# Bucket attention and two dense layers: S and the transposes of P in tiles of 64 rows

## Chip, cores and metric

The kernel runs on 1 core of one Trainium2 chip. The metric is the device time of one execution in microseconds; lower is better.

## What is computed

Attention in which a query sees only the keys of its own hash bucket, over 2 batches of 8 heads, 768 positions, head width 64; then two dense layers of width 512 and 2048. Cut to what matters:

```python
q_bits = (np.einsum('bhsd,dk->bhsk', q, proj) > 0)        # 6 bits a query, 6 a key
k_bits = (np.einsum('bhsd,dk->bhsk', k, proj) > 0)
mask   = q_bucket[:, :, :, None] == k_bucket[:, :, None, :]
scores = np.where(mask, q @ k.T / 8, -1e9)
attn   = softmax(scores); x = attn @ v                    # heads side by side: 1536 x 512
g1 = h1 * clip(h1 + 3, 0, 6) / 6, h1 = x @ w_in1;   y1 = g1 @ w_out1
g2 = h2 * tanh(softplus(h2)),     h2 = y1 @ w_in2;  out = g2 @ w_out2
```

## The kernel before

Matmul operands that must be exact to about float32 are split into a high and a low part (type fp32r) and multiplied in three products; the transposes of P and P·V take plain float32.

Attention goes over 8 pairs of heads, each with 12 *units*: 128 queries of one head against all 768 keys, 96 units in all (NU). `attention_step` (L726) writes out by hand, in program order, two units a step; every engine works through its own instructions in that order. One unit n goes through

- **S** (`emit_S`, L634): scores into two PSUM banks, one for each half of 384 keys. Each half takes two products: the first has 128 contraction rows (QA holds the high over the low part of q, KA twice the high part of k), the second 76 (QB the high part of q over 12 rows of bits, KX the low part of k over 12 rows of bits). The bits add a penalty of at least 2^30 where buckets differ. Two such pairs of banks exist, s0 and s1.
- **min** on VectorE (`emit_min`), **exp** with its sum on ScalarE (`emit_exp`), then, for four units at once, statistics on VectorE (`emit_stats`) and the normalising of P on GpSimd (`emit_norm`).
- **T** (`emit_T`, L676), L = 6 units later: six transposes of 128 x 128, three to bank t0 and three to t1; the copies to SBUF (`emit_tevac`, L690) are shared by ScalarE and VectorE.
- **P·V** (`emit_pv`, L695), 12 units later: two heads as two column tiles of 64; then the result is split into xh and xl.

A step's order on TensorE is P·V, T, S, T, S. Seen from the first T, that is T, S, T, S, P·V. `prep` (L535) makes the operands of the next pair meanwhile: high parts on GpSimd (`prep_hi`), bits by four column tiles of 32 (`prep_z`), low parts, and moves from SBUF to SBUF on SyncE's DMA queue. Lines 547 to 621 and `late_prep` are the ramp of the first pair, `busy` matmuls fill gaps there. After step n = 94 six drain steps (L806) run the last T and P·V with the first matmuls of the dense layers (`mid`) between; `HERE` (L801) is how many weight slots are opened beside attention. From there on `moe_step` runs the dense layers.

Of the kernel before, what the change touches and what calls it, by code (L numbers as in the profile page):

```python
# [20 lines left out]
def bucket_attention_two_moe_kernel(  # L21
# [50 lines left out]
    pz = const.tile([128, 32], F32, name="pz")  # L72
    c8 = const.tile([128, 8], F32, name="c8")
# [189 lines left out]
    with tc.manual_schedule():  # L263
# [153 lines left out]
        with ExitStack() as actx:  # L417
            v_p = actx.enter_context(tc.tile_pool(name="v", bufs=2, side="right"))
            p_p = actx.enter_context(tc.tile_pool(name="p", bufs=6, side="right"))
            t0_p = actx.enter_context(tc.tile_pool(name="pt0", bufs=3, side="right"))  # L420
            t1_p = actx.enter_context(tc.tile_pool(name="pt1", bufs=4, side="right"))
# [5 lines left out]
            QA = [[big.tile([128, S], F32R, name=f"qa{i}{h}") for h in range(2)] for i in range(2)]  # L427
            KA = [[big.tile([128, S], F32R, name=f"ka{i}{h}") for h in range(2)] for i in range(2)]
            QB = [[big.tile([128, S], F32R, name=f"qb{i}{h}") for h in range(2)] for i in range(2)]
            KX = [[big.tile([128, S], F32R, name=f"kb{i}{h}") for h in range(2)] for i in range(2)]  # L430
            raw_t, vn_t, bit_t, hi_t = {}, {}, {}, {}

# [4 lines left out]
            def load_first(nm):  # L437
                raw_t[0, nm] = first_tile(nm)
                nc.sync.dma_start(out=raw_t[0, nm].bitcast(F32), in_={"k": k, "q": q}[nm][0, :2].rearrange("h d s -> (h d) s"))


            def load(p):
                if p < NPAIR:
                    b, hp = divmod(p, H // 2)
                    for nm, src in (("k", k), ("q", q)):
                        t = qk_p.tile([128, S], F32R, tag=nm, name=nm)
                        nc.sync.dma_start(out=t.bitcast(F32), in_=src[b, 2 * hp:2 * hp + 2].rearrange("h d s -> (h d) s"))
                        raw_t[p, nm] = t
# [7 lines left out]
            def prep_z(p):  # L456
                if p == 0:
                    bit_t[p] = first_tile("bits")[:, :HALF]
                else:
                    bit_t[p] = qk_p.tile([128, HALF], F32R, tag="bits", name="bits")  # L460
                ps = bank("m")
                for g in range(4):
                    hf, c = divmod(g, 2)
                    P.matmul(ps[32 * g:32 * g + 32, :HALF], lhsT=pz,  # L464
                             rhs=raw_t[p, "kq"[c]].bitcast(F32)[:, hf * HALF:(hf + 1) * HALF],
                             start=True, stop=True, tile_position=(0, 32 * g))
                V.tensor_scalar(out=bit_t[p], in0=ps[:, :HALF], scalar1=0.0, scalar2=cvec,
                                op0=ALU.is_gt, op1=ALU.not_equal)

            lo_, hi_ = slice(0, 64), slice(64, 128)  # L470
            halves = [slice(0, HALF), slice(HALF, S)]
# [31 lines left out]

# [4 lines left out]
            def prep_bits(p, heads=(0, 1), groups=range(4), queue=nc.sync):  # L508
                for h in heads:
                    for g in groups:  # L510
                        hf, c = divmod(g, 2)
                        move((KX, QB)[c][p % 2][h][64:64 + NZ, hf * HALF:(hf + 1) * HALF],
                             bit_t[p][32 * g + 16 * h:32 * g + 16 * h + NZ], queue)

            def prep_q_lo(p):
                qr = raw_t[p, "q"]
                V.scalar_tensor_tensor(out=qr, in0=qr.bitcast(F32), scalar=-0.125, in1=hi_t[p][1].bitcast(F32),
                                       op0=ALU.mult, op1=ALU.subtract)
# [28 lines left out]
            load_first("k")  # L547
            with nc.allow_non_contiguous_dma(reason="tiny"):
                nc.scalar.dma_start(out=pz[lo_, :NB], in_=proj)
            load_first("q")  # L550
            A.preload_act_table_set("natural_log_exp_and_others")
            for rows, cols in ((lo_, slice(NZ, 32)), (hi_, slice(0, 16)), (hi_, slice(16 + NZ, 32))):
# [3 lines left out]
            for g in range(4):  # L556
                V.memset(kbig[32 * g:32 * g + 32], (BIG, 1.0)[g % 2])
            for g in range(8):
                o = 16 * g + (0, NB)[g // 2 % 2]
# [305 lines left out]
```

## Time and profile before

| | us |
|---|---|
| median of 3 runs | 761.95 (761.87 to 763.3) |
| profiled execution, span | 759.9 |
| first T (step n = 6) begins | 19.13 |
| steady steps, n = 12 to 94 | 32.62 to 220.86 |
| drain steps | 220.86 to 246.9 |
| dense layers alone | 246.9 to 759.9 |

How to read it: an engine's busy time in a stretch is the sum of its instructions there, overlaps counted once. The records of TensorE's matmuls overlap, since each includes its way through the array; the distance from one start to the next is what a matmul costs in a stream. "PEld" are the weight loads, which run beside the matmuls. The chain gives the time to the engine on which the end of the program hung in turn.

### The profile page before, as it was taken

The page shows a single profiled execution, that of the slowest core. Times are in us where ns is not written, and L with a number is a line of the kernel's source. Part 1 is how long each engine was busy: PE and PEld are TensorE (multiplying, and loading weights), DVE is VectorE, ACT ScalarE, POOL GpSimd, SP SyncE. Part 2 cuts the span into 40 slices and gives each one's busy share as a digit, 9 for nine tenths or more (in the row PEclk, how much of TensorE's full clock was granted, in tenths as well). Part 3 has the DMA queues.
Part 4 walks back from the last instruction along what each step waited for, and adds up shares of the span by engine and source line. Part 5 has one row for each costly group of instructions (what it writes and reads, how often), then busy time and mean ns, then how long its engine had stood idle before and what let it go on. Part 6 is the DMA issues. An engine that isn't in the chain of part 4 may idle for free.

```text
span 759.9 us, 10494 instructions
## 1 busy us (share of the span) xinstructions
PE 749.7 (99%) x3754; PEld 586.9 (77%) x3754; DVE 482.1 (63%) x907; ACT 424.1 (56%) x787; POOL 135.9 (18%) x136
## 2 busy tenths in 40 slices
PE   8899999999999999999999999999999999999997
PEld 6666666666666888888888888888888888888886
DVE  6777787787778997968566257676554756121212
ACT  6677787677868885766555245644444444222221
POOL 4666556566540000000000000000000000000000
PEclk9999999999999999999999999999999999999999
DMA  6655474665202433223212001212112110010101
GB/s 173 177 145 149 142 190 119 177 188 140 89 29 84 139 112 110 88 80 125 69 56 84 1 0 58 83 55 84 56 55 84 56 55 1 1 55 1 55 1 57
DMA packets 23236, 65.04 MB, mean 86 GB/s; under 512 B 3840, under 2 KB 5072, under 8 KB 23184
## 3 DMA queue, kind: packets, MB, share of 16 engines
q1 hardware_dynamic: 22960, 64.23, 27.5%
q8 instruction: 30, 0.49, 0.3%
q14 instruction: 22, 0.18, 0.1%
q10 hardware_dynamic: 224, 0.13, 0.1%
HBM read 42.99 MB, written 3.15 MB: 61 GB/s over the span
## 4 chain that ended last, share of the span: by engine, by line
PE 95%; DVE 2%; ACT 1%; DMA 0%; issue 0%; POOL 0%; SPq 0%; DVEq 0%; ACTq 0%; POOLq 0%
PE s L343 33%; PE t L290 17%; PE pv L290 9%; PE t L687 9%; PE s L642 8%; PE m L290 7%; PE m L700 5%; PE pv L700 4%; PE m L464 1%; PE s L290 1%; PE t L343 1%; PE m L343 1%; DVE st L650 1%; DMA q<-in_q_dram 0%; DVE pt L475 0%
## 5 line engine op out<-in xcount | busy, mean ns | idle before, releaser
L322 DVE TENSOR_TENSOR gl<-gr,gh 128x512 fp32r<-128x512 f32 x96 | 66.1, 689 | 116.6 <-PE s L343 85.1
L673 POOL TENSOR_SCALAR p<-p,st 128x768 f32<-128x768 f32 x96 | 98.0, 1036 | 75.9 <-PE t L687 34.3
L656 ACT ACTIVATE p<-s,st 128x768 f32<-128x768 f32 x96 | 86.7, 903 | 29.7 <-DVE st L650 26.8
L650 DVE TENSOR_REDUCE st<-s 128x1 f32<-128x768 f32 x96 | 91.5, 954 | 15.2 <-PE s L642 11.5
L318 ACT CAST gh<-gr 128x512 fp32r<-128x512 f32 x96 | 59.6, 621 | 61.9 <-PE s L343 37.5
L687 PEld LDWEIGHTS t<-ident,p 128*128 128x128 f32 x576 | 63.1, 140 | 37.4 <-issue 17.2
L687 PE MATMUL t<-ident,p 128*128 128x128 f32 x576 | 82.5, 278 | 2.9 <-ACT pt L474 1.7
L290 PE MATMUL t<-xh,wih 128*128 128x512 f32 x192 | 75.0, 390 | 0.0
L343 PE MATMUL s<-gh,woh 128*128 128x512 f32 x192 | 74.9, 390 | 0.0
L474 ACT COPY pt<-t 128x384 f32<-128x384 f32 x121 | 57.4, 476 | 31.1 <-PE t L687 30.5
L290 PE MATMUL t<-xl,wih 128*128 128x512 f32 x192 | 74.8, 389 | 0.0
L343 PE MATMUL s<-gh,wol 128*128 128x512 f32 x192 | 74.7, 389 | 0.0
L290 PE MATMUL t<-xh,wil 128*128 128x512 f32 x192 | 74.7, 389 | 0.0
L343 PE MATMUL s<-wol,gh 128*128 128x512 f32 x176 | 68.5, 389 | 0.0
L343 PE MATMUL s<-woh,gh 128*128 128x512 f32 x176 | 68.5, 389 | 0.0
L642 PE MATMUL s<-ka,qa 128*128 128x384 f32 x192 | 57.7, 382 | 0.4 <-DVE qa L481 0.3
L475 DVE COPY pt<-t 128x384 f32<-128x384 f32 x71 | 39.3, 554 | 29.2 <-PE t L687 29.2
L143 DVE SCALAR_TENSOR_TENSOR raw<-raw 128x512 uint32<-128x512 uint32 x64 | 44.1, 688 | 16.9 <-ACT raw L139 16.9
L642 PE MATMUL s<-kb,qb 76*128 76x384 f32 x192 | 50.2, 343 | 1.5 <-issue 1.4
L343 PE MATMUL s<-gl,woh 128*128 128x512 f32 x192 | 51.5, 389 | 0.0
L343 PE MATMUL s<-woh,gl 128*128 128x512 f32 x176 | 49.0, 389 | 0.0
L161 ACT ACTIVATE raw<-raw 128x512 f32<-128x512 uint32 x64 | 43.1, 673 | 0.6 <-DVE raw L143 0.6
(132 smaller groups left out, 1412.4 us busy)
## 6 DMA issues: line engine op xcount, KB each, us to landing
raw<-in_moe_w_in_dram SPq DMA_DIRECT2D x32, 512.0 KB
raw<-in_moe_w_out_dram SPq DMA_DIRECT2D x32, 512.0 KB
ka<-kh SPq DMA_DIRECT2D x28, 192.0 KB
k<-in_k_dram SPq DMA_DIRECT2D x8, 384.0 KB
q<-in_q_dram SPq DMA_DIRECT2D x8, 384.0 KB
vn<-in_v_dram SPq DMA_DIRECT2D x8, 384.0 KB
kb<-k SPq DMA_DIRECT2D x15, 192.0 KB
out_dram<-yp SPq DMA_DIRECT2D x11, 256.0 KB
```

Of the source, the lines that this page charges most:

```text
L143: V.scalar_tensor_tensor(out=low, in0=high, scalar=23, in1=low, op0=ALU.logical_shift_left, op1=ALU.bitwise_or)
L290: P.matmul(ps, lhsT=w[:, cs], rhs=x[t][:, c, :], start=(n == 0), stop=(n == 3 * KB - 1))
L318: A.copy(new_g(i)[0], gr_t[i])
L322: V.tensor_tensor(out=gl, in0=gr_t.pop(i), in1=gh.bitcast(F32), op=ALU.subtract)
L343: P.matmul(ys[d] if len(ys) == 4 else ys[d // 2][:, d % 2, :], lhsT=w, rhs=g, start=(j == 0 and part == 0 and n == 0), stop=(j == PARTS[ph ...
L474: acp = lambda o, i: A.copy(o, i)
L642: P.matmul(ps[:, hf, :HALF], lhsT=w[rr, qs], rhs=m[rr, hf * HALF:(hf + 1) * HALF], start=(w is QA[i][h]), stop=(w is QB[i][h]))
L650: V.tensor_reduce(out=st_t[n // 4][:, 0, n % 4:n % 4 + 1], in_=s_t[n][:, :, :HALF], op=ALU.min, axis=AX.XY)
L656: A.activation(out=pt, in_=s_t.pop(n)[:, :, :HALF], func=AF.Exp, scale=-1.0, bias=st[:, 0, n % 4:n % 4 + 1], accum_out=st[:, 1, n % 4:n % ...
L673: G.tensor_scalar(out=p_t[n], in0=p_t[n], scalar1=st[:, 3, i:i + 1], scalar2=st[:, 4, i:i + 1], op0=ALU.mult, op1=ALU.add)
L687: P.transpose(ps[:, i * 128:(i + 1) * 128], src[:, hf, i * 128:(i + 1) * 128], ident)
L700: P.matmul(pv_t[gi][64 * h:64 * h + 64, :HALF], lhsT=vn_t[p][:, h, j, :], rhs=pt_t[gi, h][j // 3][:, j % 3, :], start=(j == 0), stop=(j == ...
```

## The change

S: the array is used as two tiles of 64 rows. The keys' first half lies on rows 0 to 63 (KH, KL, BK, [128, head, 384]), the second on rows 64 to 127; q stands on both (QH, QL). Each half takes four products: high·high, low·high, high·low, and the bits, 12 rows a head in tiles of their own (BQ, BK). Each tile of rows writes its own bank. T: each 64 queries of a unit are one row tile, twelve transposes of 64 x 128 with 64 moving columns, alternating between rows and banks. A step on TensorE becomes T, S, S, (mid), T, P·V; L is 7. Both copies of the step's first T go to ScalarE, of the second one each to ScalarE and VectorE. Statistics and normalising of the last four units come first in every second step. The splitting of a finished P·V comes one step later. The moves of KA and KX are gone, those of q's parts are doubled. In the ramp q of the first pair is loaded twice in halves, its operands are made in place for both row halves with bits from `first_bk` and `first_bq` (four column tiles of 32 each, then one VectorE operation), GpSimd fills BK and BQ of the second set; eight `busy` and the later fillers stay. The diff, cut to its core:

```diff
-            p_p = actx.enter_context(tc.tile_pool(name="p", bufs=6, side="right"))
-            t0_p = actx.enter_context(tc.tile_pool(name="pt0", bufs=3, side="right"))
-            t1_p = actx.enter_context(tc.tile_pool(name="pt1", bufs=4, side="right"))
+            p_p = actx.enter_context(tc.tile_pool(name="p", bufs=7, side="right"))
+            pt_p = actx.enter_context(tc.tile_pool(name="pt", bufs=4, side="right"))
             sm_p = actx.enter_context(tc.tile_pool(name="sm", bufs=4, side="right"))
             qctx = actx.enter_context(ExitStack())
...
             def prep_hi(p):
                 i = p % 2
-                hi_t[p] = [qk_p.tile([128, S], F32R, tag=f"{nm}h", name=f"{nm}h") for nm in "kq"]
-                for t, nm, c in zip(hi_t[p], "kq", (1.0, -0.125)):
-                    G.tensor_scalar(out=t, in0=raw_t[p, nm].bitcast(F32), scalar1=c, scalar2=1.0,
-                                    op0=ALU.mult, op1=ALU.mult)
+                scaled(KH[i], raw_t[p, "k"], 1.0)
+                hi_t[p] = qk_p.tile([128, S], F32R, tag="qh", name="qh")
+                scaled(hi_t[p], raw_t[p, "q"], -0.125)
                 for h in range(2):
-                    move(KA[i][h][lo_], hi_t[p][0][hd[h]])
-                    move(KA[i][h][hi_], hi_t[p][0][hd[h]])
-                for h in range(2):
-                    move(QB[i][h][lo_], hi_t[p][1][hd[h]])
-                    move(QA[i][h][lo_], hi_t[p][1][hd[h]])
+                    for rows in both:
+                        move(QH[i][h][rows], hi_t[p][hd[h]])
...
-            def prep_bits(p, heads=(0, 1), groups=range(4), queue=nc.sync):
-                for h in heads:
-                    for g in groups:
-                        hf, c = divmod(g, 2)
-                        move((KX, QB)[c][p % 2][h][64:64 + NZ, hf * HALF:(hf + 1) * HALF],
-                             bit_t[p][32 * g + 16 * h:32 * g + 16 * h + NZ], queue)
+            def prep_bits(p):
+                i = p % 2
+                for r in range(2):
+                    for g in range(4):
+                        if g % 2:
+                            h = g // 2
+                            o = 64 * r + 16 * h
+                            e = 32 * g + 16 * r
+                            move(BK[i][o:o + NB, h], bit_t[p][e:e + NB])
+                        else:
+                            move(BQ[i][64 * r:64 * r + 16 + NZ, halves[g // 2]], bit_t[p][32 * g:32 * g + 16 + NZ])
...
             def prep_q_move(p):
                 for h in range(2):
-                    move(QA[p % 2][h][hi_], raw_t[p, "q"][hd[h]])
+                    for rows in both:
+                        move(QL[p % 2][h][rows], raw_t[p, "q"][hd[h]])
             def prep_k_lo(p):
-                kr = raw_t[p, "k"]
-                G.tensor_tensor(out=kr, in0=kr.bitcast(F32), in1=hi_t[p][0].bitcast(F32), op=ALU.subtract)
-                for h in range(2):
-                    move(KX[p % 2][h][lo_], kr[hd[h]])
+                G.tensor_tensor(out=KL[p % 2], in0=raw_t[p, "k"].bitcast(F32), in1=KH[p % 2].bitcast(F32),
+                                op=ALU.subtract)
...
+            A.copy(KH[0][:, 0], k0[:, 0].bitcast(F32))
+            first_qh(0, 0, True)
+            V.tensor_tensor(out=KL[0][:, 0], in0=k0[:, 0].bitcast(F32), in1=KH[0][:, 0].bitcast(F32), op=ALU.subtract)
+            first_bk(0, "m")
+            first_ql(0, 0)
+            first_bq(0, 0, "t0")
+            A.copy(KH[0][:, 1], k0[:, 1].bitcast(F32))
+            first_qh(1, 0, True)
+            G.tensor_tensor(out=KL[0][:, 1], in0=k0[:, 1].bitcast(F32), in1=KH[0][:, 1].bitcast(F32), op=ALU.subtract)
+            first_ql(1, 0)
...
                 ps = bank2(f"s{n % 2}")
                 i = p % 2
                 qs = slice((qh * 3 + qi) * 128, (qh * 3 + qi + 1) * 128)
-                kr = slice(0, 64 + NZ)
-                for (w, m, rr) in ((QA[i][h], KA[i][h], slice(0, 128)), (QB[i][h], KX[i][h], kr)):
-                    for hf in range(2):
-                        P.matmul(ps[:, hf, :HALF], lhsT=w[rr, qs], rhs=m[rr, hf * HALF:(hf + 1) * HALF],
-                                 start=(w is QA[i][h]), stop=(w is QB[i][h]))
+                bq = bqx if p == 0 and h == 1 else BQ[i]
+                for x, (w, m) in enumerate(((QH[i][h], KH[i]), (QL[i][h], KH[i]), (QH[i][h], KL[i]), (bq, BK[i]))):
+                    for r, rows in enumerate(both):
+                        P.matmul(ps[:, r, :HALF], lhsT=w[rows, qs], rhs=m[rows, h], start=(x == 0), stop=(x == 3))
                 s_t[n] = ps
@@ -677,20 +720,18 @@
                 p, qh, h, qi = unit(n)
                 gi = 2 * p + qh
                 if qi == 0:
-                    pt_t[gi, h] = (t0_p.tile([128, 3, HALF], F32, tag="pt0", name="pt0"),
-                                   t1_p.tile([128, 3, HALF], F32, tag="pt1", name="pt1"))
+                    pt_t[gi, h] = pt_p.tile([128, NJ, HALF], F32, tag="pt", name="pt")
                 src = p_t.pop(n)
-                tb_t[n] = []
-                for hf in range(2):
-                    ps = bank(f"t{hf}")
-                    for i in range(3):
-                        P.transpose(ps[:, i * 128:(i + 1) * 128], src[:, hf, i * 128:(i + 1) * 128], ident)
-                    tb_t[n].append(ps)
-            def emit_tevac(n, hf, cp):
+                tb_t[n] = [bank(f"t{r}") for r in range(2)]
+                for j in range(NJ):
+                    for r, rows in enumerate(both):
+                        P.transpose(tb_t[n][r][:, j * 64:(j + 1) * 64],
+                                    src[rows, j // 3, j % 3 * 128:(j % 3 + 1) * 128], ident[rows, rows])
+            def emit_tevac(n, r, cp):
                 p, qh, h, qi = unit(n)
-                cp(pt_t[2 * p + qh, h][hf][:, :, qi * 128:(qi + 1) * 128],
-                   tb_t[n][hf][:, :HALF].rearrange("p (a b) -> p a b", a=3))
+                o = qi * 128 + r * 64
+                cp(pt_t[2 * p + qh, h][:, :, o:o + 64], tb_t[n][r][:, :HALF].rearrange("p (a b) -> p a b", a=NJ))
...
+            def stats_norms(b):
+                emit_stats(b)
+                for i in range(4 * b, 4 * b + 4):
+                    emit_norm(i)
             def attention_step(n, w_act=(), w_dve=(), mid=lambda: None, between=lambda: None):
                 u = n - L
-                m = n - (L + 6)
+                m = n - 12
                 live = n < NU
+                have = [0 <= u + k < NU for k in range(2)]
+                if n % 4 == 0 and 4 < n <= NU:
+                    stats_norms(n // 4 - 1)
+                if have[0]:
+                    emit_T(u)
+                    emit_tevac(u, 0, acp)
+                    emit_tevac(u, 1, acp if live else vcp)
+                if live:
+                    emit_S(n)
+                    emit_S(n + 1)
+                mid()
+                if have[1]:
+                    emit_T(u + 1)
                 for k in (m, m + 1):
                     if 0 <= k < NU:
                         emit_pv(k // 6, k % 6)
-                for k in range(2):
-                    if 0 <= u + k < NU:
-                        emit_T(u + k)
-                    if live:
-                        emit_S(n + k)
-                    if k == 0:
-                        mid()
-                out_now = m >= 0 and m % 6 == 4
-                evac = 0 <= u < NU
-                if evac:
-                    emit_tevac(u, 0, acp)
-                if out_now:
-                    emit_pv_hi(m // 6)
+                out_gi = m // 6 if m + 2 == NU else m // 6 - 1 if m >= 6 and m % 6 == 0 else None
+                if out_gi is not None:
+                    emit_pv_hi(out_gi)
                 for part in w_act:
                     part()
-                if evac:
-                    emit_tevac(u, 1, vcp)
-                if n == 4:
+                if live:
                     emit_min(n)
-                if n % 4 == 0 and 0 < n <= NU:
-                    emit_stats(n // 4 - 1)
-                    for i in range(n - 4, n):
-                        emit_norm(i)
-                if live and n != 4:
-                    emit_min(n)
-                if evac:
+                    if n == 4:
+                        stats_norms(0)
+                    emit_exp(n)
+                    emit_min(n + 1)
+                between()
+                if have[1]:
+                    emit_tevac(u + 1, 1, vcp)
                     emit_tevac(u + 1, 0, acp)
                 if live:
-                    emit_exp(n)
-                between()
-                if evac:
-                    emit_tevac(u + 1, 1, vcp if n // 2 % 6 in (0, 3, 4) and live else acp)
-                if live:
-                    emit_min(n + 1)
                     emit_exp(n + 1)
-                if out_now:
-                    emit_pv_lo(m // 6)
-                    if m // 6 % 2 == 1 and m // 12 + 2 < NPAIR:
-                        load_v(m // 12 + 2)
+                if out_gi is not None:
+                    emit_pv_lo(out_gi)
+                    if out_gi % 2 == 1 and out_gi // 2 + 2 < NPAIR:
...
-            HERE = 7
+            HERE = 6
```

## Rows read from the trace of the kernel before

**Rows 1.** The page: TensorE's share (busy us, share, instructions), and the chain by engine.

```profile
PE 749.7 (99%) x3754; PEld 586.9 (77%) x3754; DVE 482.1 (63%) x907; ACT 424.1 (56%) x787; POOL 135.9 (18%) x136
...
PE 95%; DVE 2%; ACT 1%; DMA 0%; issue 0%; POOL 0%; SPq 0%; DVEq 0%; ACTq 0%; POOLq 0%
```

**Rows 2.** Windows: length, busy us (instructions) by engine, granted clock, DMA share, GB/s.

```profile
32.62:220.86 188.24, 188.11 (x1226) 128.20 (x1224) 147.43 (x286) 141.04 (x310) 113.68 (x108) 1.00 0.52 143
220.86:246.90 26.04, 25.96 (x139) 17.26 (x137) 19.63 (x44) 20.27 (x40) 3.89 (x4) 1.00 0.24 81
246.90:759.90 513.00, 509.02 (x2246) 420.97 (x2244) 291.69 (x525) 242.26 (x401) 0.00 (x0) 1.00 0.17 60
```

**Rows 3.** The chain in order of time, two steps: start us, us, what.

```profile
151.45 0.66 PE t L687 x6
...
154.26 0.80 PE t L687 x6
155.06 0.70 PE s L642 x4
155.76 0.82 PE t L687 x6
156.57 0.70 PE s L642 x4
157.28 1.44 PE m L700 x8
```

**Rows 4.** Timeline of TensorE, narrow stretches; then one line's durations (min/median/max).

```profile
154.79 0.30 PEld L642 LDWEIGHTS s<-ka,qa 128*128 128x128 f32 x2
...
157.21 0.20 PEld L700 LDWEIGHTS m<-pt,vn 128*64 128x64 f32 x4 [0.25 <-issue]
...
158.65 0.20 PEld L687 LDWEIGHTS t<-ident,p 128*128 128x128 f32 x2 [0.60 <-issue]
...
158.65 0.33 PE L687 MATMUL t<-ident,p 128*128 128x128 f32 x1
...
L700 PE MATMUL pv<-pt,vn x96: 486/486/537, 112.0 to 203.0; 128*64 128x384 f32 x96
```

**Rows 5.** Timeline, the bits of a pair: four column tiles, two passes.

```profile
14.01 0.51 PE L464 MATMUL m<-k,pz 128*32 128x384 f32 x1
...
14.03 0.51 PE L464 MATMUL m<-q,pz 128*32 128x384 f32 x1
14.36 0.49 PE L464 MATMUL m<-k,pz 128*32 128x384 f32 x1
...
14.01 0.11 PEld L464 LDWEIGHTS m<-k,pz 128*32 128x32 f32 x1 [0.24 <-issue]
...
14.06 0.11 PEld L464 LDWEIGHTS m<-q,pz 128*32 128x32 f32 x1
```

**Rows 6.** Timeline, a load and its matmul after a wait in the ramp.

```profile
13.47 0.19 PEld L642 LDWEIGHTS s<-kb,qb 76*128 76x128 f32 x1 [1.71 <-issue]
...
13.50 0.41 PE L642 MATMUL s<-kb,qb 76*128 76x384 f32 x1 [1.42 <-issue]
```

**Rows 7.** Groups by line, 100 to 206 us: count, busy us, mean ns, idle before.

```profile
L474 ACT COPY pt<-t 128x384 f32<-128x384 f32 x60 | 28.6, 476 | 11.7 <-PE t L687 11.3
...
L650 DVE TENSOR_REDUCE st<-s 128x1 f32<-128x768 f32 x47 | 44.8, 954 | 6.0 <-PE s L642 4.2
L475 DVE COPY pt<-t 128x384 f32<-128x384 f32 x36 | 19.9, 554 | 15.0 <-PE t L687 15.0
```

**Rows 8.** The ramp: one window, as in Rows 2, and timeline rows of first S and first T.

```profile
0.00:20.00 20.00, 16.40 (x89) 13.13 (x90) 13.13 (x38) 12.66 (x22) 10.40 (x17) 0.91 0.63 176
...
7.24 0.41 PE L642 MATMUL s<-ka,qa 128*128 128x384 f32 x1 [0.34 <-DVE qa L481]
...
19.13 0.33 PE L687 MATMUL t<-ident,p 128*128 128x128 f32 x1 [0.36 <-POOL p L673]
```

More of the change, by code (lines that the diff above doesn't have):

```diff
@@ L444, in load @@
                     b, hp = divmod(p, H // 2)
[L445 to L448, printed above, removed]
+                    raw_t[p, "k"] = qk_p.tile([128, 2, HALF], F32R, tag="k", name="k")
+                    load_k(p, raw_t[p, "k"])
+                    raw_t[p, "q"] = qk_p.tile([128, S], F32R, tag="q", name="q")
+                    nc.sync.dma_start(out=raw_t[p, "q"].bitcast(F32),
+                                      in_=q[b, 2 * hp:2 * hp + 2].rearrange("h d s -> (h d) s"))
             def load_v(p):
@@ L545, in busy, with load_q0 @@
                     P.matmul(idle[:, :128], lhsT=ident, rhs=ident, start=True, stop=True)
-            load_first("k")
+            k0 = first_tile("k0").rearrange("p (h t) -> p h t", h=2)
+            q0 = [first_tile(f"q0{h}") for h in range(2)]
+            bqx = first_tile("bqx")
+            qn = first_tile("qn")
+            def load_q0(h, hf, queue):
+                for rows in both:
+                    queue.dma_start(out=q0[h][rows, halves[hf]].bitcast(F32), in_=q[0, h, :, halves[hf]])
             with nc.allow_non_contiguous_dma(reason="tiny"):
                 nc.scalar.dma_start(out=pz[lo_, :NB], in_=proj)
-            load_first("q")
+            load_k(0, k0)
+            load_q0(0, 0, nc.scalar)
+            load_q0(1, 0, nc.sync)
             A.preload_act_table_set("natural_log_exp_and_others")
-            for rows, cols in ((lo_, slice(NZ, 32)), (hi_, slice(0, 16)), (hi_, slice(16 + NZ, 32))):
+            for hf, h in ((1, 0), (1, 1)):
+                load_q0(h, hf, nc.sync)
+            for rows, cols in ((lo_, slice(NZ, 32)), (lo_, slice(32 + NZ, 48)), (hi_, slice(0, 16)),
+                               (hi_, slice(16 + NZ, 48))):
                 V.memset(pz[rows, cols], 0.0)
@@ new lines, in bucket_attention_two_moe_kernel @@
+            V.tensor_scalar(out=c8[:, 4:8], in0=c8[:, 0:4], scalar1=BIG, scalar2=None, op0=ALU.mult)
+            for h in range(2):
+                V.scalar_tensor_tensor(out=c8[:, 8 + h:9 + h], in0=c8[:, 4 + 2 * h:5 + 2 * h], scalar=-2.0,
+                                       in1=c8[:, 5 + 2 * h:6 + 2 * h], op0=ALU.mult, op1=ALU.add)
+                V.tensor_scalar(out=c8[:, 10 + h:11 + h], in0=c8[:, 1 + 2 * h:2 + 2 * h], scalar1=-3e38, scalar2=None,
+                                op0=ALU.mult)
@@ L599, in bucket_attention_two_moe_kernel, with z_all @@
-            G.tensor_tensor(out=k0[hi_], in0=k0[hi_].bitcast(F32), in1=KA[0][1][hi_].bitcast(F32), op=ALU.subtract)
-            prep_bits(0, (1,), (0, 2, 1))
-            move(KX[0][1][lo_], k0[hi_])
-            prep_bits(0, (1,), (3,))
+            def z_all(tag, x, turned=()):
+                ps = bank(tag)
+                for g in range(4):
+                    o = 16 if g in turned else 0
+                    P.matmul(ps[32 * g:32 * g + 32, :HALF], lhsT=pz[:, o:o + 32], rhs=x.bitcast(F32),
+                             start=True, stop=True, tile_position=(0, 32 * g))
+                return ps[:, :HALF]
@@ L789, in bucket_attention_two_moe_kernel @@
                 attention_step(n, *w_at.get(n // 2, ((), ())),
[L790 removed]
+                               between=lambda: None)
                 if n < 6:
@@ L808, in bucket_attention_two_moe_kernel @@
             u = 2 * PRE
-            for n, (pe, g, pushes) in zip(range(NU, NU + L + 6, 2), drain):
+            for n, (pe, g, pushes) in zip(range(NU, NU + 12, 2), drain):
                 attention_step(n, mid=pe)
```

128 lines of the change are left out of this document (68 added, 60 removed).

## The prediction

> **What bounds the kernel now.** I read the page first, by engine and then the chain that ended last [rows 1]: TensorE is busy 99% of the span and carries 95% of the chain, so time can only go where TensorE's own queue gets shorter. Then the span cut into stages [rows 2]: the 42 steady attention steps take 188.24 us, that is 4.48 us a step, with TensorE busy all of it, VectorE 147.43 (3.51 a step), ScalarE 141.04 (3.36) and GpSimd 113.68 (2.71). The drain takes 26.04 us and the two dense layers 513.00, at TensorE 99%; the change touches nothing in the latter. So the question is the step. The chain in order of time [rows 3] gives its pieces: transposes of one unit 0.80, S 0.70, transposes 0.82, S 0.70, P·V 1.44, sum 4.46. In the step before, the second transpose piece was 0.66; I take the 0.16 between them as a wait for a PSUM bank. A clean step is 0.80 + 0.70 + 0.66 + 0.70 + 1.44 = 4.30, so 0.18 of the mean step is waits and the bits' matmuls of each pair; I keep that 0.18.
>
> What a piece is made of: six transposes in 0.66 are 0.110 apiece. That is not the weight load, since two loads end 0.20 after the first began, each lasting 0.14 [rows 4], so a second load can start 0.06 after the first. The 0.110 is therefore the 128 moving columns. Four S products of 384 columns in 0.70 are 0.175 apiece; their weight loads are 0.11 apart (two of 0.19 in 0.30) [rows 4] and hidden. The first transpose piece is 0.14 longer than the clean second: a change of tile shape after P·V.
>
> **Transposes.** Before: 6 of 128 moving columns. After: 12 of 64 rows and 64 moving columns, two side by side on the two array halves. If the halves run together, a unit is 6 pairs, each the longer of half of 0.110 (0.055) and one load (0.06): 0.36 in place of 0.66, 0.30 saved a unit, 0.60 a step. Whether row halves run together no row of before shows; the nearest are column tiles. Eight P·V matmuls of 0.49 each fill 1.44, and four of their loads fit in 0.20 [rows 4], as two loads of the full array do. The bits' four column tiles start within 0.02 and their second pass 0.35 later, with eight loads begun within 0.05 [rows 5]. Bounds: 0.36 a unit (together) to 12 × 0.06 = 0.72 (loads in single file). I take the lower, as the column tiles do just that.
>
> **S.** Before: four products of 128 (or 76) rows. After: eight of 64 rows, in four pairs on two banks, 384 columns each: 4 × 0.175 = 0.70, no change. Columns are not saved, since the rows that were empty in the second product are now spent on a third and fourth. Loads of a pair, together, are 0.11 under a 0.175 stream. Bounds 0.70 to 8 × 0.11 = 0.88 if loads go in single file; I take 0.70. One thing is added: the first S load behind a transpose of 0.055 is no longer covered, 0.11 − 0.055 = 0.05 once a step.
>
> **Order.** T, S, S, T, P·V in place of T, S, T, S, P·V. The tile shape changes twice a step as before (P·V to T, T to P·V). The wait before the second T (0.16 at worst) goes, because two S lie between, 1.4 us, against two ScalarE copies of 0.48 [rows 7]. What it newly does: P·V of a group's first step needs the copies of that step's first T; two copies end about 1.1 after T, and S, S, T take 1.75, so this is covered by 0.6.
>
> Clean step after: 0.80 − 0.30 + 0.05 + 0.70 + 0.70 + 0.36 + 1.44 = 3.75; with the 0.18 kept, 3.93.
>
> **The instruction stream.** A step now has 24 + 16 + 8 = 48 load-and-matmul pairs in place of 28. Where TensorE's queue had run empty behind a wait, a load begins at 13.47 and its matmul at 13.50 [rows 6]; where it was full, both begin at 158.65 [rows 4]. So issuing costs about 0.03 an instruction, 0.06 a pair: 48 pairs are 2.9 us of a 3.93 step. It fits on average, but a T that starts with an empty queue takes 12 × 0.06 = 0.72 in place of 0.36. Each T begins with waits (normalised p, two banks), and those stop the issue. The second T has 1.4 us of S ahead of it; the first waits for the bank that ScalarE empties after exp, late in the step. Bounds: 0 to 0.72 a step. I take 0.13, a third of one T, because most of P·V's 1.44 is there to fill the queue. The Trainium skill, "TensorE: Matmul & The Clock Gate", section "Wait — 56ns, not 53.3ns?", puts ≈62 ns on every matmul where the sequencer's microcode decodes it; by that rule alone both T are 0.74, the step 4.69 and the time 768, slower. The rows agree with it for an empty queue and not for a full one, where four matmuls begin in 0.02 [rows 5].
>
> **The other engines.** Copies out of the transposes go from 2.5 on ScalarE and 1.5 on VectorE a step to 3 and 1, at 0.476 and 0.554 [rows 7]: ScalarE 3.36 + 0.24 = 3.60, VectorE 3.51 − 0.28 = 3.23. GpSimd keeps its four preparation operations a pair. SyncE issues 16 moves and 3 loads a pair in place of 20 and 2; fewer bytes, and nothing of it is on the chain. Statistics now stand at the head of VectorE's queue in every second step, waiting for the last exp; behind them is the next minimum, which needs S of this step, 1.2 later, so it is covered. Normalising has half a step more before its T.
> A loop over VectorE could decide: S 0.70, two minima of 0.95, a copy of 0.55, T 0.36, and hops: 3.5 to 3.9. It is just under the step.
>
> Step: 3.93 + 0.13 = 4.06, against 4.48: 0.42 × 42 = 17.6 us. Ends: 0.55 × 42 = 23.1 with no issue loss; nothing with all of it (4.65 would even lose 7).
>
> **Drain.** Seven T at −0.30 are −2.1; a dense product of full rows now stands between two T of half rows, six changes of shape at 0.14, +0.8. Net −1.3. One weight slot fewer fits beside attention; its first use is later than the drain, and I cost it at 0, up to +1 if that load is then waited for.
>
> **Ramp.** The first S starts at 7.24, the first T at 19.13, and the granted clock of the first 20 us is 0.91 [rows 8]: so a part of it went at 1.2 GHz instead of 2.4, where TensorE had little to do. New: q comes twice from HBM in halves, no copies across partitions for the first pair, four more fills and shifts on GpSimd, more small matmuls. Neither cost has its row; I bound it by −3 (the wait of a second head's operands gone) and +3, and take −1 with the three steps that already have a T.
>
> **Sum.** 759.9 − 17.6 − 1.3 − 1 = 740.0 on the profiled span. The median of the runs is 761.95, 2.05 above the span, so 742.
>
> **Rivals.**
> 1. *Issue bound.* The first T of each step starts with an empty queue and the second partly: 0.36 to 0.72 on the step, 4.3 to 4.65. For it: [rows 6]. Against: average need of 2.9 in 3.9. Time 752 to 767; from 0.57 on the step it is within 0.2% of before, from 0.64 slower. Chance 0.18, of it 0.03 within and 0.04 slower.
> 2. *Other engines take over.* ScalarE at 3.60 needs 0.04 of gap at each of some ten instructions to reach 4.0, and the VectorE loop may be 3.9; with the extra work of weights and preparation a step would be 4.2: 42 × 0.28 = 11.8, time about 748. Chance 0.17.
> 3. *Slower: array halves do not load side by side.* If loads of the two row halves go in single file, T is 0.72 and S 0.88: 3.93 + 2 × 0.36 + 2 × 0.18 = 5.01 a step, +22 us, about 784; it turns slower once a pair costs more than about 0.1 in T. If the matmuls too were in file, S would be 1.40, a step 6.0, time above 820. Against: column tiles do both side by side. In a sentence of its own: the Trainium skill, "TensorE: Matmul & The Clock Gate", Part 3, reports four row tiles of 32 rows 3.07 times as fast, which speaks against this rival; no run here shows it yet. Chance 0.08.
> 4. *Nothing lost.* No issue loss and a ramp 2 us shorter: 733. Chance 0.10.
>
> **How the numbers follow.** The forecast (736 to 747) has 0.47. About 0.2% (1.5 us) is what a measurement of this kernel tells from no change. Slower: rival 3 and the end of rival 1, 0.12; same, rival 1's, 0.03; faster, the rest, 0.85. The range leaves out rival 3 above, the last of rival 1, and below only what beats rival 4: 729 to 764.
>
> **What would show it.** Right: transposes' six pairs in the chain at about 0.36, pair members starting within 0.02, S unchanged at 0.70, a step near 4.06. Issue bound: loads and matmuls of T 0.03 apart one after the other. Rival 2: TensorE idle in the steady stage, put down to ScalarE or VectorE. Rival 3: pair members 0.06 (T) or 0.11 (S) apart and no overlap. The prediction is wrong if S moves by more than 0.1 or the ramp by more than 3 us.

## The result, and the profile after

The changed kernel takes **753.11 us** (median of 4 runs, 752.57 to 754.79); the kernel before, timed beside it, 762.62 (761.87 to 763.48). The ratio is 0.9877, 95% interval 0.9859 to 0.9895. So it is faster by 9.5 us, where 20 were forecast: the direction is right, the size is half. The profiled execution took 754.79, the longest of the four; its span is 753.0, where the others have 750.8 to 751.7. The profile of before, 759.9, is one of its shortest executions (later ones had 759.9 to 763.2). So the two profiles lie 6.9 apart and the medians 9.5.

The page of after, with TensorE's share and then the chain by engine, answers to [rows 1]:

```profile
PE 731.3 (97%) x4754; PEld 576.3 (77%) x4754; DVE 473.8 (63%) x893; ACT 419.9 (56%) x802; POOL 137.7 (18%) x141
...
PE 81%; DVE 9%; ACT 4%; issue 2%; POOL 1%; DMA 1%; SPq 1%; DVEq 0%; ACTq 0%; POOLq 0%
```

TensorE was 95% of the chain and is 81%; VectorE and ScalarE have 13% where they had 3%. TensorE now waits. The windows tell where (columns as in [rows 2]). The stages run from the first instruction of step n = 12 on TensorE to that of n = 96, and on to the first matmul after the drain; first two lines of before cut at these points, then two of after:

```profile
31.18:219.42 188.24, 188.11 (x1225) 128.20 (x1224) 147.05 (x285) 140.84 (x310) 113.68 (x108) 1.00 0.52 144
219.42:249.79 30.37, 30.29 (x157) 20.10 (x157) 23.82 (x51) 24.05 (x47) 3.89 (x4) 1.00 0.27 87
```

```profile
34.42:212.58 178.16, 166.47 (x2064) 117.72 (x2065) 136.54 (x266) 140.84 (x330) 112.97 (x108) 1.00 0.48 125
212.58:243.11 30.53, 30.35 (x204) 19.24 (x205) 25.07 (x55) 22.94 (x43) 3.88 (x4) 1.00 0.27 87
```

| us | forecast | profiled, after less before |
|---|---|---|
| ramp, to n = 12 | -1 | 34.42 - 31.18 = +3.2 |
| 42 steady steps | -17.6 | 178.16 - 188.24 = -10.1 |
| drain | -1.3 | 30.53 - 30.37 = +0.2 |
| dense layers | 0 | 509.9 - 510.1 = -0.2 |
| span | -19.9 | -6.9 |

The ramp is what differs between executions; how much of its +3.2 is the program's is worked out below, under the run without fillers.

In the steady stage TensorE is idle for 178.16 - 166.47 = 11.7 us; before, for 0.1. Two pieces of the chain in order of time (start, length, what; answer to [rows 3]) show both what the change brought and what took part of it back:

```profile
107.19 0.59 PE t L728 x12
107.78 1.47 PE s L686 x16
109.25 0.37 PE t L728 x12
109.62 1.44 PE m L741 x8
111.06 0.07 issue
111.13 0.59 PE t L728 x12
...
118.73 1.11 issue
119.84 0.06 DVE bits L470
...
120.37 0.95 DVE q L518
121.32 0.08 DVE st L706
...
122.21 0.88 DVE st L693
...
123.17 0.84 ACT p L699
...
124.06 0.48 ACT pt L474
...
124.68 0.59 PE t L728 x12
```

A clean step is 107.19 to 111.13, 3.94: T 0.59, two S 1.47, T 0.37, P·V 1.44, and 0.07 of waiting. The second T is the 0.36 that was forecast and S is unchanged. The lower part is a stall that comes once in each pair of heads. The step that begins when P·V and the bits' matmuls are over (119.64 on TensorE) runs its own pieces, but the next one begins only at 124.68, 5.03 later. In between VectorE makes the bits, then the low part of q (0.95), then the statistics, and only then the minimum; exp waits for that, and behind exp on ScalarE stands the copy that frees the bank of the next T.

The steps, from the start of one first T to the next, repeat with the pair: 3.94, 4.58 (the one with the bits' matmuls), 5.03 (the stall), 3.94, 3.94 to 4.35, 3.94. Against the 3.79 that TensorE's own pieces need (0.52 + 1.46 + 0.37 + 1.44, where nothing waits; shown below) the 42 steps lose 178.16 - 159.2 = 19.0: 0.15 in every step (6.3), six stalls of 1.09 (6.5), the bits' matmuls 0.64 six times (3.8), and 2.4 in single steps.

### The profile page after: what moved, and what is told of

The parts are those of the page before. It is cut to its first block, busy times and chain, and to the rows that moved or that the text cites. A ratio compares the mean times of both kernels' runs of the same rounds, so it can differ in the third digit from the quotient of the medians.

```text
span 753.0 us, 12408 instructions
## 1 busy us (share of the span) xinstructions
PE 731.3 (97%) x4754; PEld 576.3 (77%) x4754; DVE 473.8 (63%) x893; ACT 419.9 (56%) x802; POOL 137.7 (18%) x141
## 4 chain that ended last, share of the span: by engine, by line
PE 81%; DVE 9%; ACT 4%; issue 2%; POOL 1%; DMA 1%; SPq 1%; DVEq 0%; ACTq 0%; POOLq 0%
PE s L343 33%; PE t L290 17%; PE pv L290 9%; PE m L290 7%; PE s L686 5%; DVE st L693 4%; PE t L728 3%; ACT p L699 2%; PE pv L741 2%; PE m L741 2%; ACT pt L474 1%; DVE q L518 1%; PE s L290 1%; DMA qh<-qh 1%; PE t L343 1%
## 5 line engine op out<-in xcount | busy, mean ns | idle before, releaser
L693 DVE TENSOR_REDUCE st<-s 128x1 f32<-128x768 f32 x96 | 87.7, 951 | 32.2 <-PE s L686 32.0
L728 PEld LDWEIGHTS t<-ident,p 64*128 64x128 f32 x1152 | 50.8, 139 | 45.6 <-POOL p L716 24.6
L728 PE MATMUL t<-ident,p 64*128 64x64 f32 x1152 | 56.0, 226 | 14.6 <-ACT pt L474 12.3
L474 ACT COPY pt<-t 128x384 f32<-128x384 f32 x140 | 62.6, 484 | 9.7 <-PE t L728 9.7
L139 ACT ACTIVATE raw<-raw 128x512 uint32<-128x512 uint32 x64 | 43.2, 674 | 0.0
L290 PEld LDWEIGHTS t<-xh,wih 128*128 128x128 f32 x192 | 36.1, 188 | 8.7 <-issue 1.2
L310 ACT ACTIVATE gr<-t 128x512 f32<-128x512 f32 x24 | 14.4, 599 | 49.8 <-PE t L290 46.8
```

Source lines behind the costliest of these rows:

```text
L139: A.activation(out=low, in_=low, func=AF.Copy, scale=(1.0 - 2.0 ** -22) * 2.0 ** -9)
L290: P.matmul(ps, lhsT=w[:, cs], rhs=x[t][:, c, :], start=(n == 0), stop=(n == 3 * KB - 1))
L474: acp = lambda o, i: A.copy(o, i)
L693: V.tensor_reduce(out=st_t[n // 4][:, 0, n % 4:n % 4 + 1], in_=s_t[n][:, :, :HALF], op=ALU.min, axis=AX.XY)
L728: P.transpose(tb_t[n][r][:, j * 64:(j + 1) * 64], src[rows, j // 3, j % 3 * 128:(j % 3 + 1) * 128], ident[rows, rows])
```

## Experiments

The **theory**: the tiles do what they should, and what is missing of the gain is (a) the stall behind q's low part on VectorE, (b) a loop min, exp, copy, T, S that holds a clean step at 3.94, (c) `busy` fillers and waits in the ramp. The **rival**: the shape of the tiles costs the time, either in S or in the issue of 48 loads and matmuls a step. The kernel before took 762.57 beside four of the experiments (the low part of q later, T back to full rows, the two single ones of the ramp) and 762.41 beside the other four, medians of 7 runs each; each experiment has 4 runs.

### The low part of q one step later

```diff
-            PREP = ((), (prep_hi, prep_z, prep_scale, prep_q_lo), (prep_bits, prep_q_move), (prep_k_lo,),
+            PREP = ((), (prep_hi, prep_z, prep_scale), (prep_bits, prep_q_lo, prep_q_move), (prep_k_lo,),
```

> The changed kernel with one edit in the steady stage: VectorE's prep_q_lo (0.95) goes from the second step of each pair to the third, where no statistics follow at the head of the next step. In the changed kernel the step from the second to the third of every pair is 5.03 us and the others 3.93 to 4.6; in that one the chain goes bits, q_lo, statistics, minimum, exp, copy, T. Theory 'VectorE's queue, not TensorE, sets that step': 5.03 becomes 4.0 to 4.3 in 7 pairs and the next step grows by 0 to 0.3, so the time falls by 4 to 7 us, to 746 to 749. Rival 'ScalarE is the bound, or the bits themselves, which wait for TensorE behind P.V': the 0.9 shows up in the next step or stays, and the time stays within 1.5 of 753.

Measured: 748.98 (745.77 to 750.09), ratio 0.9812, interval 0.9783 to 0.9841. The chain at the same place:

```profile
118.08 0.62 DVE bits L470
118.69 0.07 DVE st L706
```

Statistics follow the bits at once, the 5.03 step is 4.01, all others stay, and the 42 steps take 172.03 in place of 178.16. (a) is shown, and it is worth 6.1 us of the steady stage. The medians differ by 4.1; in this profile n = 12 came 1.3 later than in that of after.

### ScalarE copies before exp

```diff
+                if have[1]:
+                    emit_tevac(u + 1, 0, acp)
+                if live:
                     emit_exp(n)
                     emit_min(n + 1)
                 between()
                 if have[1]:
                     emit_tevac(u + 1, 1, vcp)
-                    emit_tevac(u + 1, 0, acp)
```

> The changed kernel with one edit: on ScalarE the copy out of the second T's bank t0 stands ahead of the first exp of the step instead of behind it. In the changed kernel even the clean steps (3.94) run in a loop minimum, exp, copy, T: exp from 113.56, the copy from 114.45 to 114.92, T at 115.07, while P.V ended at about 115.0; and the first T then issues from an empty queue, a matmul every 0.03, 0.52 for the unit instead of 0.37. Theory 'the copy behind exp sets the step and empties TensorE's queue': the first T takes about 0.37 to 0.45, clean steps fall to 3.75 to 3.85, the 5.03 step falls by 0.3 to 1.0 too, the time by 4 to 10 us to 743 to 749. Rival 'TensorE is the bound of the clean step': steps stay within 0.05 of 3.94 and the time within 2 of 753 (or exp comes later and it is slower).

Measured: 747.28 (746.61 to 750.06), ratio 0.9809, interval 0.9788 to 0.983. The chain:

```profile
106.75 0.52 PE t L728 x12
107.27 1.45 PE s L686 x16
108.72 0.37 PE t L728 x12
109.08 1.44 PE pv L741 x8
```

In the clean steps TensorE works without a break, 3.78 a step; (b) is shown. The stall has only moved: one step of each pair is 4.8, behind the same low part of q. The 42 steps take 173.45, 4.7 less than after; the medians differ by 5.8.

### Only T back to full rows

The copies out of the banks follow the new place of their columns; the diff is cut to the transposes.

```diff
-                for j in range(NJ):
-                    for r, rows in enumerate(both):
-                        P.transpose(tb_t[n][r][:, j * 64:(j + 1) * 64],
-                                    src[rows, j // 3, j % 3 * 128:(j % 3 + 1) * 128], ident[rows, rows])
+                for r in range(2):
+                    for j in range(3):
+                        P.transpose(tb_t[n][r][:, j * 128:(j + 1) * 128], src[:, r, j * 128:(j + 1) * 128], ident)
...
```

> The changed kernel with the transposes alone put back: six of 128 x 128 a unit instead of twelve of 64 x 128; S stays in 64-row tiles, order and lags stay. Theory of the prediction: a unit's transposes take 0.66 again (+0.30), 0.60 a step, and the tile shape changes at T-S and S-T too, two more changes of about 0.14, so a clean step grows from 3.93 to 4.5 to 4.85. With some of it taken from waits the time grows by 20 to 35 us, to 773 to 788. Rival 'the gain lies in the order (S, S together, copies off the path), not in the narrower transposes': the step stays under 4.2 and the time under 760.

Measured: 776.97 (776.68 to 777.34), ratio 1.0186, interval 1.0168 to 1.0204: slower than before. The chain:

```profile
109.96 0.81 PE t L728 x6
110.77 1.59 PE s L686 x16
112.36 0.81 PE t L728 x6
113.17 1.44 PE m L740 x8
```

Both T cost 0.81 and the two S 1.59, together 4.65, as expected. The order alone does not make the gain.

### Only T in half rows, in the kernel before

The same twelve transposes in the kernel before, with its S, its order and its lag of 6; one buffer for each head's transposed P, since each bank now holds half of the queries, and one weight slot fewer beside attention, as in the changed kernel. The diff is cut to the transposes.

```diff
-                for hf in range(2):
-                    ps = bank(f"t{hf}")
-                    for i in range(3):
-                        P.transpose(ps[:, i * 128:(i + 1) * 128], src[:, hf, i * 128:(i + 1) * 128], ident)
-                    tb_t[n].append(ps)
+                tb_t[n] = [bank(f"t{r}") for r in range(2)]
+                for j in range(NJ):
+                    for r, rows in enumerate((lo_, hi_)):
+                        P.transpose(tb_t[n][r][:, j * 64:(j + 1) * 64],
+                                    src[rows, j // 3, j % 3 * 128:(j % 3 + 1) * 128], ident[rows, rows])
...
```

> The kernel before with the transposes alone changed to twelve of 64 x 128 a unit (one P-transposed tile a head as in the changed kernel, one weight slot fewer beside attention); S stays at 128 and 76 rows, order and lags stay. Theory: 0.60 a step saved in the transposes, but the tile shape now changes at T-S, S-T, T-S and S-P.V, three more changes than before at 0.10 to 0.15: a clean step of 4.31 becomes 4.0 to 4.2, time 750 to 757. Rival 'shape changes cost nothing (what was read as one is a weight load)': clean step 3.7 to 3.9, time below 748. Rival 'shape changes cost more than 0.2': no gain, 760 or more.

Measured: 779.29 (778.64 to 782.08), ratio 1.0229, interval 1.0203 to 1.0254. The theory's 750 to 757 failed; the second rival's 760 or more came. The chain of a clean step, then of the step behind it:

```profile
113.05 0.52 PE t L684 x12
113.57 0.89 PE s L641 x4
114.46 0.52 PE t L684 x12
114.98 0.91 PE s L641 x4
115.89 1.44 PE m L698 x8
...
118.74 0.56 PE t L684 x12
119.30 0.47 ACT pt L473
...
120.83 0.38 ACT pt L473
...
121.25 1.50 PE pv L698 x6
```

Two things go wrong. A T alone between two S of full rows is 0.52, not 0.37, and each S behind it is 0.90 where it was 0.70 [rows 3]: the step is 4.28, as good as before's 4.31. And P·V of a group's first step now needs both banks, so it waits for the copy that ScalarE makes behind exp, 1.1 to 1.3 us twice a pair. A pair of heads takes 28.9 in place of 26.9; seven of them make 14 of the 17 us.

### Only the order, in the kernel before

The step of the changed kernel (statistics first, T, S, S, T, P·V, its copies, lag 7, seven tiles of P, one weight slot fewer beside attention) with S and T of before. The diff is cut to TensorE's order.

```diff
-                for k in range(2):
-                    if 0 <= u + k < NU:
-                        emit_T(u + k)
-                    if live:
-                        emit_S(n + k)
-                    if k == 0:
-                        mid()
+                if have[0]:
+                    emit_T(u)
+                    emit_tevac(u, 0, acp)
+                    emit_tevac(u, 1, acp if live else vcp)
+                if live:
+                    emit_S(n)
+                    emit_S(n + 1)
+                mid()
+                if have[1]:
+                    emit_T(u + 1)
...
```

> The kernel before with the order and the lags alone of the changed kernel (T, S, S, T, P.V; lag 7; three copies on ScalarE and one on VectorE; statistics first; 7 tiles of P; one weight slot fewer); S and T keep 128 rows, the ramp is the old one. Theory of the prediction: TensorE's work stays 4.30 a step, waits of at most 0.16 go: 4.25 to 4.45 a step, time 755 to 763. Rival 'the order makes the gain': below 752. Rival 'the order costs, by the copy behind exp and the statistics first': over 765.

Measured: 765.67 (765.58 to 765.68), ratio 1.0043, interval 1.0028 to 1.0058. The chain:

```profile
106.26 0.81 PE t L687 x6
107.06 1.43 PE s L642 x8
108.49 0.66 PE t L687 x6
109.15 1.44 PE m L700 x8
```

Clean steps are 4.29 to 4.33, TensorE's pieces and no more, so the loop (b) does not show under a step of this length; but one step of each pair is 5.06, the same stall. So the theory's 755 to 763 was missed and the rival that the order costs (over 765) came, if by little: 3.3 us, of them 2.7 in the steady steps. The stall belongs to the order: before, with its own, has no such step.

The four clean steps stand in a square. All four are free of waits (the fourth is the experiment with the copies ahead of exp):

| TensorE's pieces of a clean step | S with full rows | S in halves |
|---|---|---|
| T with full rows | 0.81 + 1.43 + 0.66 + 1.44 = 4.34 | 0.81 + 1.59 + 0.81 + 1.44 = 4.65 |
| T in halves | 0.52 + 0.89 + 0.52 + 0.91 + 1.44 = 4.28 | 0.52 + 1.45 + 0.37 + 1.44 = 3.78 |

One half of the change alone loses 0.3 or gains 0.06; both together gain 0.56. The lower left one has before's order T, S, T, S, and with it one border from T to S more than T, S, S, T would have; T in halves in that order would be about 0.52 + 1.43 + 0.2 + 0.52 + 1.44 = 4.1, an estimate from these pieces that no run shows. A border between two tile shapes costs 0.15 where T comes behind another shape (0.81 against 0.66, 0.52 against 0.37) and 0.16 to 0.2 where S comes behind one. The whole step says so too, wherever one piece is taken to end: with two borders more it is 4.65 against 4.34. P·V stands behind another shape in every run, so no run shows a price for it.

### The ramp: q's low part earlier, and no fillers

The second half of head 1's q parts ahead of GpSimd's other work at n = 2:

```diff
                     prep_hi(1)
+                    first_qh(1, 1, False)
+                    first_ql(1, 1)
                     prep_scale(1)
...
                     busy(3)
-                    first_qh(1, 1, False)
-                    first_ql(1, 1)
```

> The changed kernel, with one edit in the ramp: GpSimd makes the high and low part of the second head's second half of q (first_qh and first_ql of (1, 1)) behind prep_hi(1) instead of behind the first four normalisings. In the changed kernel GpSimd had nothing from 12.5 to 19.5 us, then the first normalisings to 24.85, then these operands until 27.58; the second product of unit 9 began at 27.64, and TensorE went to the lower clock from 30.4. Theory 'the ramp lost 7.4 us, and about 3 of it hang on this place in GpSimd's queue': the first T of step n = 12 comes at 36 to 37.5 instead of 38.57, S of unit 9 no longer waits for GpSimd, the time is 750 to 752 against 753.1. Rival 'the ramp is late because the first operands are late (first S at 10.48 against 7.24), and the wait at unit 9 only hides later waits': step n = 12 at 38.2 to 38.6, 753.

Measured: 753.69 (753.35 to 755.91), ratio 0.989, interval 0.9865 to 0.9916: no gain. From the first T to n = 12 are 11.3 us in its profile and 10.9 in that of after; n = 12 comes at 32.95 against 34.42, but the first T had come earlier already (21.62 against 23.56). This part of (c) falls. The expectation took the step at 38.57 for n = 12. That is n = 14, so the ramp of that profile had lost 3.2 us and not 7.4.

The two groups of fillers ahead of the first and the third S left out:

```diff
             first_ql(1, 0)
-            busy(4)
...
                     first_qh(0, 1, False)
-                    busy(6)
```

> The changed kernel without the filler matmuls ahead of the first S (4) and ahead of the third S (6). They ran from 8.75 to 10.3 and from 13.50 to 14.9, and S followed them at 10.48 and 15.04, although its operands were there at about 9.5 and s0 was free at 13.4. Theory 'fillers stand in the way': the first S begins at 9.0 to 9.6, the third S at about 12.5 to 13.5, the time is 1 to 2.5 us shorter, 751. Rival 'the fillers keep the clock': TensorE gets 1.2 GHz for a longer stretch of the ramp (mean of the first 40 us below 0.9) and the time is the same or up to 2 us longer, 753 to 755.

Measured: 751.5 (749.95 to 752.45), ratio 0.985, interval 0.9828 to 0.9872, 1.6 below after, though the two intervals overlap a little. The first matmuls of the bits, the wait ahead of them and the fillers, first in after, then in this one (count, ns min/median/max, first and last start; "idle until" in us, times):

```profile
L603 PE MATMUL m<-k,pz x8: 818/845/847, 6.0 to 6.7; 128*32 128x384 f32 x8
...
  DMA k<-in_k_dram: 0.9, 1
...
L545 PE MATMUL pv<-ident x20: 274/275/582, 8.7 to 14.8; 128*128 128x128 f32 x20
```

```profile
L603 PE MATMUL m<-k,pz x8: 487/556/636, 5.7 to 6.2; 128*32 128x384 f32 x8
```

In after TensorE waits 0.9 for k, its matmuls then take 845 ns, and the first S stands behind 8 fillers that begin only at 8.7: it starts at 10.48. Without them it starts at 7.25, as before (7.24 [rows 8]), and n = 12 comes at 31.57, against 34.42. But the same matmuls were slow in one execution and quick in the next: with the fillers in, n = 12 came between 31.8 and 35.7 in the profiles of after and of the experiments that leave the ramp's fillers alone. The granted clock of 6.0 to 8.7 us is 1.00 in both profiles, so it does not say why they were slow. A stretch at the lower clock is another thing that comes and goes: in after the granted clock is 0.58 from 30 to 34 us, so for most of it 1.2 GHz and not 2.4, behind 10 us in which TensorE was busy for 6.75; in the profile with the copies ahead of exp it is 1.00 in each stretch up to 40 us.

An estimate parts the program from the execution. After and the two experiments of the ramp are the same program from n = 12 on, and from there to the end their profiles take 718.6, 718.6 and 718.5. If their other executions take as much, the spans of after (median 751.3) put n = 12 at 32.7, and those without fillers (median 749.7) at 31.2. The same for before, 728.7 and a median span of 760.8, gives 32.1. So the program's ramp is about 0.6 longer than before's with the fillers and 0.9 shorter without; the rest of the 3.2 lies in the two profiled executions, of which after's is long and before's short.

### All three

The low part of q later, ScalarE's copy ahead of exp, and no fillers, with no other edit.

> The changed kernel with three edits that were or are run alone: q_lo a step later (alone 749.0 against 753.1), the copy of t0 ahead of exp, and no fillers ahead of the first and third S (alone 751.5). If the parts add up and the copy brings 4 to 8: 739 to 744. If the copy ahead of exp brings nothing by itself: 746 to 748. If VectorE or ScalarE becomes the bound of every step (3.3 and 3.6 us of work), the steady step stays at 3.95 or more and the time at 745 or more.

Measured: **741.76** (739.85 to 742.86), ratio 0.9727, interval 0.9708 to 0.9746; the best of all. The chain:

```profile
108.03 0.52 PE t L726 x12
108.55 1.46 PE s L684 x16
110.01 0.37 PE t L726 x12
110.38 1.44 PE pv L739 x8
```

The 42 steps take 168.38, 4.01 each; a step is TensorE's own pieces (3.78 to 3.81, and 4.58 with the bits' matmuls), save for one of 3.8 to 4.4 in each pair and four of 3.9 to 4.4 in the last.

## Why the prediction was right, and where it was wrong

On the medians 10.5 us of the forecast gain are missing: 7.5 in the steady steps (4.24 a step where 4.06 was forecast), 1.5 in the drain, and, by the estimate above, about 1.6 in the ramp. TensorE's pieces came as forecast; what failed was mainly the account of who waits for whom.

**TensorE's pieces: right.** T 0.36 was forecast, 0.37 measured behind S; the first T 0.80 - 0.30 = 0.50, measured 0.52; S 0.70 a unit plus 0.05, measured 1.45 to 1.47 for two; P·V 1.44. The clean step of 3.75 is 3.78 where nothing waits.

**The issue loss: over-sized.** 0.13 was taken, at most 0.72. The first T, which comes from an empty queue, takes 0.59, and 0.52 where the queue is full: 0.07. The mistake is in the reading of [rows 6]: 0.03, the distance from a load to its matmul, was taken as the price of one instruction. Two narrow stretches of after, the loads of a T from an empty queue and the matmuls of one from a full queue:

```profile
107.16 0.20 PEld L728 LDWEIGHTS t<-ident,p 64*128 64x128 f32 x3 [1.05 <-POOL p L716]
...
109.09 0.46 PE L728 MATMUL t<-ident,p 64*128 64x64 f32 x9
```

Three loads of 0.14 fit in 0.20, so they begin 0.03 apart, each with its matmul in between; the price is at most 0.03 for load and matmul together. Nine matmuls of 0.22 in 0.46 are as many: 0.03 apart on the mean. Rival 1 is out. So is the time by the ≈62 ns that the Trainium skill ("TensorE: Matmul & The Clock Gate", section "Wait — 56ns, not 53.3ns?") gives for a matmul decoded by microcode: twelve are 0.74 by it, an estimate, and T is 0.37 to 0.59 here.

**Rival 3 is out**: sixteen S matmuls of half the rows take 1.46, about as long as eight of full rows (1.43). **Rival 4**, 733 with nothing lost, is reached by no run: the best has 741.76.

**Steady steps: the step of the argument that failed.** "The other engines" said that the statistics at the head of VectorE's queue wait for the last exp and that what is behind them "needs S of this step, 1.2 later, so it is covered". That weighed only one instruction of the queue. Once a pair the low part of q (0.95) and the bits (0.6) stand ahead of the statistics, and the bits wait 1.1 until their matmuls on TensorE, behind P·V, are out; then min 0.95, exp 0.9 and a copy of 0.47 follow one after the other before T may start. That is the 5.03 step: 6.5 us, of which moving one operation gave back 6.1. The forecast kept 0.18 a step for waits, which is 7.6 in all; what was found beyond the bits' matmuls (3.8) and single steps (2.4) is this stall (6.5) and the loop (6.3).

The loop is the second place. The prediction wrote one down over VectorE, with two minima and VectorE's copy, 3.5 to 3.9, and called it "just under the step", a step of 4.06 that held an issue loss which did not come. TensorE's own pieces are 3.79, and the loop that held goes through one minimum, exp and the copy that ScalarE makes behind exp: 3.94. With that copy ahead of exp the step is 3.78.

Rival 2 had the step right: it said 4.2, and 4.24 was measured, for the reason it named in part, "the VectorE loop may be 3.9" (3.94). It had a chance of 0.17, and its 748 kept the forecast's ramp and drain, which did not come. The counts of busy time were no help: ScalarE's 140.84 in the steady steps is the same in both kernels, 3.35 a step and not the 3.60 that was worked out, and still it stood in the chain.

Statistics and low part were in before's steps too. There a step of TensorE's 4.31 and another place in VectorE's queue covered them. In before the low part ran from 149.19 to 150.14, and VectorE then had nothing to do until TensorE's next T was out:

```profile
150.79 0.56 DVE L475 COPY pt<-t 128x384 f32<-128x384 f32 x1 [0.65 <-PE t L687]
```

With the new order and before's tiles the stall is there (5.06).

**The single operations** cost what was said (ScalarE's copy 0.49 where it was 0.48); the minimum's group, 100 to 206 us, answers to [rows 7]:

```profile
L693 DVE TENSOR_REDUCE st<-s 128x1 f32<-128x768 f32 x50 | 45.5, 951 | 15.9 <-PE s L686 15.8
```

It waits for S, as in [rows 7]; its place in the loop matters, and its length is the same.

**Drain: mis-sized.** Seven T at 0.30 less were put in, and six changes of shape at 0.14. But before has six T there; the seventh comes from the lag of 7, so it is a cost and no saving. The chain of before, a dense product behind a T of full rows, and of after, a T, a product, a T:

```profile
227.38 2.74 PE s L290 x12
```

```profile
218.07 0.52 PE t L728 x12
218.59 3.01 PE s L290 x12
221.60 0.56 PE t L728 x12
```

Where nothing waits, every T is 0.52 to 0.56, and the product is 2.94 to 3.01, where it was 2.74. Seven T at 0.52 are 3.6, against six at 0.81 or 0.66 (4.4), a gain of 0.8 where 2.1 was put in; most of the miss is the seventh T. The products behind T take that 0.8 back at 0.2 to 0.27 each. The forecast had the price of the border ahead of T about right (0.14, measured 0.15), and the one behind it, ahead of a product of full rows, too low.

**Ramp: mis-sized**, by 4.2 in the profile and by about 1.6 on the medians (the estimate above). The forecast called a ramp that moves by more than 3 a sign that it is wrong, and the profile's moved by 3.2. It took no account of the fillers, which stay in TensorE's order while the operands of S change; the medians put them at 1.6, as much as is missing. Nor did it reckon with k's coming later, or with executions whose ramps differ by up to 4; why they do stays open.

With the stall, the loop and the fillers gone the time is 741.76, beside a forecast of 742; two errors of opposite sign stand behind that: the steady steps gained 19.9 where 17.6 were forecast, and the drain nothing where 1.3 were. So that 742 was hit is in part luck; it confirms the pieces, and not each term.

## What to carry to other kernels

When a bounding engine's step gets shorter, write out the next engine's queue for the one step in which the rare operations come, and add up everything between its first wait and the result that the bounding engine needs; the mean busy share does not show it. Count the borders between tile shapes before changing one shape alone: here S alone lost 0.3 a step, T alone, in an order with one border more, gained 0.06, and the two together gained 0.56. Moving one line can then be worth much: two such lines gave 9.8 of the steady stage's 19.9 us.

## What the runs showed of the hardware

Two tiles of 64 rows run side by side in transposes (0.66 to 0.37 for the same data) and in S (sixteen in 1.46). From an empty queue, load and matmul together are issued every 0.03 us. A border between tile shapes costs TensorE 0.15 to 0.2 us from full rows to half rows and back, 0.52 against 0.37 for T and 0.90 against 0.70 for S, and 0.2 to 0.27 on a dense product; so the way from half rows back to full ones costs no less. The Trainium skill, "TensorEngine Tiling (Array Packing)", section "Key Properties", says that changing the tiling mode drains the engine, without a figure. The borders above agree with it; that their time is this drain, and not something else that comes with a border, no run shows.
